# Keeping 15 instead of 12 squared-score blocks per sequence in an attention, FFN and channel-mix kernel

## The chip, the core and the metric

The program runs on one core of a Trainium2 chip. The metric is the device time of one execution in microseconds (us). The engines are TensorE (PE in the profile, its weight loads PEld), VectorE (DVE), ScalarE (ACT), GpSimd (POOL, idle here) and SyncE (SP), which issues almost all DMAs and does it in order: a DMA that waits for an engine holds up every DMA behind it. The time of the kernel before is the median of three runs, 2616.7 us (2616.6 to 2617.11).

## The reference

Three layers follow each other over 4 sequences of 3072 tokens with 256 features; z has 64 features.

```python
scores = scale * np.matmul(z, z.transpose(0, 2, 1))
attn = np.maximum(scores, 0.0) ** 2
out = np.matmul(attn, v)
x = u * out                              # attention
h = x @ w_in
x = (h - np.tanh(h)) @ w_out             # FFN, d_ff 2048
xk = mu_k * x + (1.0 - mu_k) * x_prev    # x_prev: the token before
xr = mu_r * x + (1.0 - mu_r) * x_prev
k = np.maximum(xk @ w_k, 0.0)            # channel mix, d_ff 1024
out = 1.0 / (1.0 + np.exp(-(xr @ w_r))) * (k * k @ w_v)
```

The scores are symmetric: the block of queries g and keys i is the transpose of the block of queries i and keys g.

## The kernel before

**Tiles and units.** Tokens are cut into 24 tiles of 512 (`t`, six for each of the 4 sequences, `g` is the place in the sequence). A unit is a pair of 128-row chunks. The attention has 24 x 12 units `("A", t, p)`, and 12 key pairs `kp` make up six blocks of 512 keys. The units of the FFN (`H`) and of the channel mix (`K`, `R`) follow. Loop `n` does `produce(units[n])` and then `consume(units[n - 2])` (`LAG = 2`).

**Precision.** Every operand is split into a high part `h` (a copy in fp32r by `copy_hi` on ACT or a cast on DVE) and a low part `l` (a subtraction on DVE, `sub_lo`), and a product takes three matmuls.

**A fresh attention unit** takes 4 matmuls into PSUM tile `w` (lines 428 and 429), a Relu (line 339) and a Square (line 340) on ACT into `a`, the high and the low part, and later 12 matmuls into `acc` (line 500).

**A kept unit.** For query tile g the first `min(g, 3)` key blocks are not computed again. The tile with the smaller index stored the squared block (`keep`, line 370, 512 KB for each pair), and `again_load` (line 377) fetches it as four DMAs of 256 KB, 7 units before its first use. `turn` (line 402) turns it with two 32x32-block transposes on DVE, `turned_high` copies the high part on ACT, and the low part follows. Such a unit has no matmuls in `produce`, only the 12 of `consume`. In tiles with g < 3 the query columns stand in another order (`swapped`, `columns`), which costs a copy `zq` of each such z tile.

**What sets the order.** Every engine works in the order in which the program is written. Other work (z, v, u and weight preparation) is cut into steps with a cost, a first and a last unit. `run_steps(n)` puts in as many as a budget `left` allows. The weights come as 64-bit floats and are rebuilt on DVE by `c_steps` during the attention.

**Pools.** Tile tag `p4` has 10 buffers and holds raw loads, u, x1 and weights under way, `e` has 4 and holds `a`, `big` has 12 and holds v, fetched blocks and weights, `hi` and `lo` have 3 each, PSUM `wk` 2.

Of the kernel before, what the change touches and what calls it, by code (L numbers as in the profile page):

```python
# [7 lines left out]
F32 = mybir.dt.float32  # L8
F32R = mybir.dt.float32r
# [10 lines left out]
def relu2_attention__tanh_ffn__channel_mix_kernel(  # L20
# [23 lines left out]


# [13 lines left out]
    AGAIN = 3  # L59
# [39 lines left out]
    zin, z1, zq, z2, vraw, vs, uin, uT = {}, {}, {}, {}, {}, {}, {}, {}  # L99
# [78 lines left out]
    def u_turn(t):  # L178
        a = uin.pop(t)
        w = p4(f"uT{t}")  # L180
        if t % NG < AGAIN:
            for c in range(DC):
                nc.vector.transpose(
                    out=w[:, c].rearrange("p (b a i) -> p b a i", a=4, b=4),
                    in_=a[:, c].rearrange("p (a b) i -> p b a i", a=4),
                )
        else:
            nc.vector.transpose(
                out=w.rearrange("p c t -> p (c t)"), in_=a.rearrange("p c k i -> p (c k i)")
            )  # L190
        uT[t] = w
# [142 lines left out]
    def square_split(name, w, sc, pieces=1, high=nc.vector.tensor_copy, beside=None):  # L334
        a = scratch(f"a_{name}")
        h, l = parts(name)
        for j in range(pieces):
            x = slice(2 * j // pieces, 2 * (j + 1) // pieces)
            nc.scalar.activation(out=a[:, x], in_=w[:, x], func=ACTF.Relu, scale=sc)  # L339
            nc.scalar.activation(out=a[:, x], in_=a[:, x], func=ACTF.Square)  # L340
            if j == 0 and beside:
                beside()
            high(h[:, x], a[:, x])  # L343
            sub_lo(l[:, x], a[:, x], h[:, x])
        return a, h, l


    again = {g: range(min(g, AGAIN)) for g in range(NG)}
    fresh = {g: [j for j in range(NG) if j not in again[g]] for g in range(NG)}
    pairs = {}  # L350
    for g in range(NG):
        of_f = [2 * j + h for j in fresh[g] for h in range(2)]
        of_r = [2 * j + h for j in again[g] for h in range(2)]
        if g == 1:
            of_f = of_f[2:] + of_f[:2]
        if len(of_r) == 2:
            pairs[g] = of_f[:8] + [of_r[0], of_f[8], of_r[1], of_f[9]]
        elif len(of_r) == 4:
            pairs[g] = [x for i in range(4) for x in (*of_f[2 * i : 2 * i + 2], of_r[i])]
        elif of_r:  # L360
            pairs[g] = [x for i in range(6) for x in (of_f[i], of_r[i])]
        else:
            pairs[g] = of_f
# [4 lines left out]
    def keep(b, g, kp, a):  # L368
        rows = kept[b, g, kp // 2][kp % 2 * 2 * P : (kp % 2 + 1) * 2 * P, :]
        nc.sync.dma_start(out=rows.rearrange("(c p) q -> p c q", p=P), in_=a)  # L370

    def again_load(b, g, i):

        t = sb.tile([P, 16, 4 * 32], F32, tag="big", name=f"b{b}_{g}_{i}", bufs=12)
        src = kept[b, i, g].rearrange("(m j) (q x) -> q j m x", j=32, q=4)
        for q in range(4):
            nc.sync.dma_start(out=t[32 * q : 32 * q + 32], in_=src[q])
        blocks[b, g, i] = t

    def is_again(n):  # L380
        if n >= NT * NP:
            return False
        g, q = n // NP % NG, n % NP
        return pairs[g][q] // 2 in again[g]

    def turn(n):
# [5 lines left out]
        x = blocks[b, g, kp // 2]  # L392
        a = scratch(f"t_{t}_{q}")
        for j in range(2):
            f = kp % 2 * 2 + j
            y = x[:, :, f * 32 : f * 32 + 32]
            if g < AGAIN:
                y = y.rearrange("p (c k) i -> p k c i", c=4)
                o = a[:, j].rearrange("p (k c i) -> p k c i", k=4, c=4)
            else:  # L400
                o = a[:, j].rearrange("p (m i) -> p m i", i=32)
            nc.vector.transpose(out=o, in_=y)
        turned[n] = a

    def turned_high(n):
        if n in turned:
            h, l = parts("t_{}_{}".format(*divmod(n, NP)))
            copy_hi(h, turned[n])
            turned[n] = (turned[n], h, l)

    def produce(unit):
# [3 lines left out]
        if n in turned:  # L415
            a, h, l = turned.pop(n)
            sub_lo(l, a, h)
            split[unit] = (h, l)
            return
        w = work(f"w_{name}")  # L420
        if kind == "A":
            turn(n + 1)
            b, g = divmod(t, NG)
            kp = pairs[g][p]
            for j in range(2):
                kc = 2 * kp + j
# [3 lines left out]
            a, *split[unit] = square_split(  # L430
                name, w, scale, 2 if t == 0 and p == 0 else 1,
                copy_hi if g > 1 else nc.vector.tensor_copy, lambda: run_steps(n),
            )
            if (b, g, kp // 2) in kept:
                stores[n + 1] = lambda: keep(b, g, kp, a)
        elif kind in ("H", "K"):
# [15 lines left out]
            if kind == "K":  # L452
                _, *split[unit] = square_split(name, w, 1.0)
# [31 lines left out]
    def consume(unit):  # L485
# [6 lines left out]
        for j in range(2):  # L492
            f = 2 * (pairs[t % NG][p] if kind == "A" else p) + j
# [22 lines left out]
    def x2_steps(i):  # L516
        def f():
            o = acc.pop(("H", i))
            x2t[i] = []
            for c in range(DC):  # L520
                x = p2(f"x2_{i}_{c}")
                if i % NG < AGAIN:
                    nc.scalar.activation(out=columns(x), in_=swapped(o[:, c]), func=ACTF.Copy)
                else:
                    nc.scalar.activation(out=x, in_=o[:, c], func=ACTF.Copy)
# [105 lines left out]
    for b in range(1, B):  # L631
        prev = (b - 1) * NG * NP
        last = prev + (NG - 1) * NP
        for g in range(NG):
            n = prev + (3 + g) * NP if g < 3 else last + 3 + LAG + (1, 2, 5)[g - 3]
            load(n, v_load, b, g)
            task(n + 3, min(n + 12, b * NG * NP + 2 * g + LAG - 2), v_steps, b, g)
        for g in range(NG):
            n = last - 3 * NP // 2 + 3 * g if g < 3 else last + 2 * (g - 3) + 2
            load(n - 3, z_load, b, g)  # L640
            task(n, b * NG * NP + 2 * g - 1 if g else b * NG * NP - 5, z_steps, b, g)
    for t in range(NT):
        b, g = divmod(t, NG)
        for i in again[g]:
            load(t * NP + pairs[g].index(2 * i) - 7, again_load, b, g, i)
    order = [(k, g) for g in range(F1 // 512) for k in ("in", "out")]
    order += [(k, g) for k in ("k", "v") for g in range(F2 // 512)] + [("r", 0)]
    halves = [(k, g, h) for k, g in order for h in range(1 if k == "r" else 2)]
    c0 = NP + 2
    c1 = (NT - NG) * NP  # L650
    for n, x in enumerate(halves):
        k = c0 + n * (c1 - c0) // len(halves)
        load(k - 3, c_load, *x)
        task(k, k + 2 * (c1 - c0) // len(halves), c_steps, *x)
# [22 lines left out]
    def run_steps(n):  # L677
# [20 lines left out]
    with tc.manual_schedule():  # L698
# [10 lines left out]
        for n in range(len(units) + LAG + 3):  # L709
# [8 lines left out]
            turned_high(n + 1)  # L718
# [37 lines left out]
```

## Time and profile before

| | us |
|---|---|
| median of three runs | 2616.7 |
| the profiled execution, its own time | 2616.88 |
| its span, first to last instruction | 2615.1 |
| PE busy | 2595.5 (99%) |
| DVE busy | 1669.4 (64%) |
| ACT busy | 1387.9 (53%) |

The 1.8 us between the span and the time lie around the first and the last instruction. The attention takes the first 980 us or so, in which the DVE is much busier than after it. A busy share is an average, and whether an engine limits the kernel is read from who waits for it.

### The profile page before, as it was taken

How to read it: one execution, taken by the hardware profiler on the slowest of the kernel's cores; microseconds unless marked ns; L12 is line 12 of the kernel's file. 1: busy time of each engine (PE TensorE's matmuls, PEld its weight loads, DVE VectorE, ACT ScalarE, POOL GpSimd, SP SyncE). 2: the span in 40 equal slices, each digit the busy share in tenths (PEclk: the TensorE clock that was granted, in tenths of full speed). 3: DMA queues.
4: the chain of work that ended last, by engine and by line, in shares of the span. 5: the costliest groups of instructions: out<-in, count | busy, mean ns of one | idle time of the engine just before them, and what ended most of it. 6: DMA issues, size and time to landing. Idle time of an engine off the chain costs nothing.

```text
span 2615.1 us, 28460 instructions
## 1 busy us (share of the span) xinstructions
PE 2595.5 (99%) x11424; PEld 2146.2 (82%) x11424; DVE 1669.4 (64%) x1880; ACT 1387.9 (53%) x1502; POOL 0.2 (0%) x4
## 2 busy tenths in 40 slices
PE   8999999999999999999999999999999999999998
PEld 6888888888888888888888888888888888888887
DVE  7888888887886666555555555555555555555554
ACT  6666666656666665444444444444444444444443
POOL 0000000000000000000000000000000000000000
PEclk9999999999999999999999999999999999999999
DMA  8685777578657630000000000000000000000000
GB/s 209 203 211 132 231 196 175 153 205 221 151 162 210 139 112 33 15 12 12 17 15 14 17 17 17 17 17 17 17 17 17 17 17 17 17 17 17 17 9 17
DMA packets 415604, 203.99 MB, mean 78 GB/s; under 512 B 261488, under 2 KB 372080, under 8 KB 415472
## 3 DMA queue, kind: packets, MB, share of 16 engines
q1 hardware_dynamic: 414416, 202.04, 30.3%
q8 instruction: 89, 1.46, 0.2%
q14 instruction: 43, 0.35, 0.0%
q10 hardware_dynamic: 1056, 0.13, 0.0%
HBM read 114.03 MB, written 82.05 MB: 75 GB/s over the span
## 4 chain that ended last, share of the span: by engine, by line
PE 99%; DVE 1%; ACT 0%; DMA 0%; issue 0%; ACTq 0%; DVEq 0%
PE acc_A L500 30%; PE acc_H L500 20%; PE w_H L444 20%; PE acc_K L500 10%; PE w_K L444 10%; PE w_A L428 3%; PE w_A L429 3%; PE w_R L468 2%; DVE z L96 0%; DMA zin<-in_z_dram 0%; DVE zt L118 0%; ACT zq L93 0%; DVE l_A L96 0%; ACT h_A L93 0%; DVE z L119 0%
## 5 line engine op out<-in xcount | busy, mean ns | idle before, releaser
L500 PE MATMUL acc_A<-h_A,v 128*128 128x512 f32 x1536 | 504.0, 390 | 0.0
L500 PE MATMUL acc_H<-h_H,w_out 128*128 128x512 f32 x1536 | 504.0, 389 | 0.0
L444 PE MATMUL w_H<-xh,w_in 128*128 128x512 f32 x1536 | 500.4, 389 | 0.0
L93 ACT ACTIVATE h_H<-g_H 128x1024 fp32r<-128x1024 f32 x192 | 203.7, 1061 | 386.3 <-DVE g_H L458 386.3
L96 DVE TENSOR_TENSOR l_H<-g_H,h_H 128x1024 fp32r<-128x1024 f32 x192 | 235.4, 1226 | 216.3 <-ACT h_H L93 216.3
L339 ACT ACTIVATE a_A<-w_A 128x1024 f32<-128x1024 f32 (+1 forms) x193 | 197.7, 1024 | 300.3 <-PE w_A L429 294.1
L458 DVE TENSOR_TENSOR g_H<-w_H,g_H 128x1024 f32<-128x1024 f32 x192 | 233.6, 1217 | 171.3 <-ACT g_H L457 171.3
L500 PEld LDWEIGHTS acc_A<-h_A,v 128*128 128x128 f32 x1536 | 289.1, 188 | 60.1
L500 PEld LDWEIGHTS acc_H<-h_H,w_out 128*128 128x128 f32 x1536 | 288.3, 188 | 59.8
L444 PEld LDWEIGHTS w_H<-xh,w_in 128*128 128x128 f32 x1536 | 288.3, 188 | 59.8
L457 ACT ACTIVATE g_H<-w_H 128x1024 f32<-128x1024 f32 x192 | 195.8, 1020 | 243.3 <-PE w_H L444 243.1
L96 DVE TENSOR_TENSOR l_A<-a_A,h_A 128x1024 fp32r<-128x1024 f32 (+1 forms) x193 | 235.4, 1219 | 128.7 <-ACT h_A L93 125.1
L500 PE MATMUL acc_A<-l_A,v 128*128 128x512 f32 x768 | 299.9, 391 | 0.0
L444 PE MATMUL w_H<-x,w_in 128*128 128x512 f32 x768 | 298.8, 389 | 0.0
L500 PE MATMUL acc_H<-l_H,w_out 128*128 128x512 f32 x768 | 298.8, 389 | 0.0
L500 PE MATMUL acc_A<-h_t,v 128*128 128x512 f32 x768 | 252.0, 389 | 0.0
L444 PE MATMUL w_K<-mkh,w_k 128*128 128x512 f32 x768 | 251.8, 389 | 0.0
L500 PE MATMUL acc_K<-h_K,w_v 128*128 128x512 f32 x768 | 251.8, 389 | 0.0
L340 ACT ACTIVATE a_A<-a_A 128x1024 f32<-128x1024 f32 (+1 forms) x193 | 204.0, 1057 | 6.1
L343 DVE CAST h_K<-a_K 128x1024 fp32r<-128x1024 f32 x96 | 66.7, 695 | 212.8 <-ACT a_K L340 212.8
L339 ACT ACTIVATE a_K<-w_K 128x1024 f32<-128x1024 f32 x96 | 98.8, 1029 | 136.8 <-PE w_K L444 134.5
L500 PEld LDWEIGHTS acc_A<-l_A,v 128*128 128x128 f32 x768 | 144.6, 188 | 32.3 <-DVE l_A L96 2.1
(127 smaller groups left out, 3484.6 us busy)
## 6 DMA issues: line engine op xcount, KB each, us to landing
at<-a_A SPq DMA_DIRECT2D x96, 512.0 KB, 3.4
b<-at SPq DMA_DIRECT2D x192, 256.0 KB, 4.8
vr<-in_v_dram SPq DMA_DIRECT2D x24, 512.0 KB, 5.5
uin<-in_u_dram SPq DMA_DIRECT2D x192, 64.0 KB, 2.7
x1d<-x SPq DMA_DIRECT2D x24, 512.0 KB, 3.1
x<-x1d SPq DMA_DIRECT2D x24, 512.0 KB, 3.8
out_dram<-ot SPq DMA_DIRECT2D x192, 64.0 KB, 1.9
zin<-in_z_dram SPq DMA_DIRECT2D x94, 64.0 KB, 2.7
```

The lines of the kernel that those rows point to most:

```text
L93: nc.scalar.activation(out=o, in_=i, func=ACTF.Copy)
L96: nc.vector.tensor_tensor(out=o, in0=i, in1=hi.bitcast(F32), op=ALU.subtract)
L339: nc.scalar.activation(out=a[:, x], in_=w[:, x], func=ACTF.Relu, scale=sc)
L340: nc.scalar.activation(out=a[:, x], in_=a[:, x], func=ACTF.Square)
L343: high(h[:, x], a[:, x])
L428: nc.tensor.matmul(w[:, j], lhsT, zq[b, g], start=True, stop=False)
L429: nc.tensor.matmul(w[:, j], lhsT, z2[t], start=False, stop=True)
L444: nc.tensor.matmul(w[:, j], ws[wt, f // 4][a][:, c, (f % 4) * P : (f % 4 + 1) * P], x[m][:, c], start=n == 0, stop=n == 3 * DC - 1,)
L457: nc.scalar.activation(out=g, in_=w, func=ACTF.Tanh)
L458: nc.vector.tensor_tensor(out=g, in0=w, in1=g, op=ALU.subtract)
L468: nc.tensor.matmul(w[:, d], ws["r", 0][a][:, c, d * P : (d + 1) * P], x[m][:, c], start=n == 0, stop=n == 3 * DC - 1,)
L500: nc.tensor.matmul(o[:, c], w[a][:, c * P : (c + 1) * P], s[m][:, j], start=p == 0 and j == 0 and n == 0, stop=p == last and j == 1 and n ...
```

## The change

For query tile g all g lower blocks are now kept, 15 instead of 12 for a sequence. The tile that computes a block turns it with two DVE transposes into a `p4` tile and stores that, so that a fetch brings rows of 1 KB to a group of 32 partitions. The user of a block does no transposes: ACT copies the high part and DVE subtracts, each as two instructions of 512 columns. A pair `kp` now stands for chunks 0 and 2 or 1 and 3 of a block. The swapped column order and the `zq` copies are gone. The sequence of fresh and kept units is written as strings, fetches go out 5 units ahead instead of 7, the high cast stands on ACT more often, loads and steps of z, v and weights have other places, and the weight conversion spreads over more of the attention.

```diff
-    AGAIN = 3
+    AHEAD = 5
...
-    kept = {(b, i, g): dr.tile([TB, TB], F32, name=f"at{b}_{i}_{g}")
-            for b in range(B) for g in range(NG) for i in again[g]}
-    stores, blocks, turned = {}, {}, {}
...
+        ("ffffffffffff", "ffffrfrfffff", "ffrffrffrffr", "frfrfrfrfrfr", "rfrrfrrfrrfr", "rrfrrrrrfrrr")
...
+    kept = {(b, i, g): dr.tile([2 * P, 1024], F32, name=f"at{b}_{i}_{g}")
+            for b in range(B) for g in range(NG) for i in range(g)}
...
+    def keep(n, b, g, kp, a):
...
+        t = p4(f"k{b}_{g}_{kp}", shape=(P, 4, 4, 2, 32))
+        for c in range(2):
+            nc.vector.transpose(
+                out=t[:, :, :, c].rearrange("p b a j -> p a b j"),
+                in_=a[:, c].rearrange("p (a b i) -> p a b i", a=4, b=4),
+            )
...
+        def store():
+            rows = kept[b, g, kp // 2][kp % 2 * P : (kp % 2 + 1) * P, :]
+            nc.sync.dma_start(out=rows, in_=t.rearrange("p b a c j -> p (b a c j)"))
+            stored.add((b, g, kp))
...
+        stores[n + 1] = store
...
+        t = sb.tile([P, 8, 256], F32, tag="big", name=f"b{b}_{g}_{i}", bufs=12)
+        src = kept[b, i, g].rearrange("(m i) (q x) -> q i m x", i=32, q=4)
...
+        for hj, lj, xj in turned[n][0]:
+            copy_hi(hj, xj)
...
+            for hj, lj, xj in views:
+                sub_lo(lj, xj, hj)
...
-                nc.tensor.matmul(w[:, j], lhsT, zq[b, g], start=True, stop=False)
+                nc.tensor.matmul(w[:, j], lhsT, z1[b, g], start=True, stop=False)
...
+            def beside(a):
+                run_steps(n)
+                if kept_on:
+                    keep(n, b, g, kp, a)
...
+                nc.vector.tensor_copy if n < 3 or not g and p % 3 == 2 else copy_hi, beside,
...
+        left = {"A": 2.0, "H": 2.2, "K": 2.4, "R": 4.0}[kind] + spare[0]
+        if kind == "A":
+            t, q = divmod(n, NP)
+            j = pairs[t % NG][q] // 2 - t % NG
+            left -= 1.0 if j < 0 else 1.1 if j > 0 else 0.0
```

On DVE, in the first tile at units 3 and 4, the program before has a cast and a subtraction for each unit and the preparation of a z tile between them (`a`, `h`, `l` are the squared scores and their parts, the last number but one is the unit):

```order
L343 CAST h_A_3_270<-a_A_3_269 128x1024
L96 TENSOR_TENSOR l_A_3_271<-a_A_3_269,h_A_3_270 128x1024
L118 STREAM_TRANSPOSE zt_4_304<-zin_4_258 128x512
L119 CAST z_0_4_305<-zt_4_304 128x512
L96 TENSOR_TENSOR z_0_4_305<-zt_4_304,z_0_4_305 64x512
L343 CAST h_A_4_300<-a_A_4_299 128x1024
L96 TENSOR_TENSOR l_A_4_301<-a_A_4_299,h_A_4_300 128x1024
```

The same place in the changed program, `k` being the turned tile that is stored:

```order
L341 STREAM_TRANSPOSE k_0_3_286<-a_A_3_278 128x4x4x32 x2
L87 TENSOR_TENSOR l_A_3_280<-a_A_3_278,h_A_3_279 128x1024
L341 STREAM_TRANSPOSE k_0_4_316<-a_A_4_311 128x4x4x32 x2
L87 TENSOR_TENSOR l_A_4_313<-a_A_4_311,h_A_4_312 128x1024
L109 STREAM_TRANSPOSE zt_4_358<-zin_4_267 128x512
L110 CAST z_0_4_359<-zt_4_358 128x512
L87 TENSOR_TENSOR z_0_4_359<-zt_4_358,z_0_4_359 64x512
```

Two transposes have taken the place of the cast ahead of each subtraction, and two casts in three have gone to ACT.

On DVE, in the second tile, which uses the first kept block `b`, the program before turns it (`t`) and subtracts:

```order
L402 STREAM_TRANSPOSE t_8_763<-b_1_0_582 128x512 x2
L183 STREAM_TRANSPOSE uT_775<-uin_573 128x512 x2
L343 CAST h_A_7_771<-a_A_7_770 128x1024
L96 TENSOR_TENSOR l_A_7_772<-a_A_7_770,h_A_7_771 128x1024
L96 TENSOR_TENSOR l_t_8_793<-t_8_763,h_t_8_792 128x1024
```

In the changed program a kept unit (`l_t`) is two subtractions, and the fresh units beside it have the transposes:

```order
L341 STREAM_TRANSPOSE k_1_5_691<-a_A_3_682 128x4x4x32 x2
L87 TENSOR_TENSOR l_A_3_684<-a_A_3_682,h_A_3_683 128x1024
L87 TENSOR_TENSOR l_t_4_709<-b_1_0_547,h_t_4_708 128x512 x2
L218 TENSOR_SCALAR c_r_0_552<-cw_r_0_687 128x512
L221 TENSOR_TENSOR cw_r_0_687<-cw_r_0_687,c_r_0_552 128x512
L222 TENSOR_SCALAR cw_r_0_687<-cw_r_0_687 128x512
L341 STREAM_TRANSPOSE k_1_6_740<-a_A_5_732 128x4x4x32 x2
L87 TENSOR_TENSOR l_A_5_734<-a_A_5_732,h_A_5_733 128x1024
```

The transposes have moved from the tile that uses a block to the tile that computes it.

On ACT, at the very start of the program before, the three copies `zq` stand among the first unit's Relu (line 339) and Square (line 340):

```order
L93 ACTIVATE zq_0_162<-z_0_0_158 128x512
L93 ACTIVATE z_0_164<-zt_0_157 64x512
L93 ACTIVATE zq_1_172<-z_0_1_168 128x512
L93 ACTIVATE v_0_174<-vr_0_148 128x1024
L339 ACTIVATE a_A_0_186<-w_A_0_181 128x512
L340 ACTIVATE a_A_0_186<-a_A_0_186 128x512
L93 ACTIVATE zq_2_196<-z_0_2_192 128x512
L339 ACTIVATE a_A_0_186<-w_A_0_181 128x512
L340 ACTIVATE a_A_0_186<-a_A_0_186 128x512
```

In the changed program they read:

```order
L84 ACTIVATE z_0_174<-zt_0_169 64x512
L84 ACTIVATE v_0_182<-vr_0_160 128x1024
L318 ACTIVATE a_A_0_194<-w_A_0_189 128x512
L319 ACTIVATE a_A_0_194<-a_A_0_194 128x512
L318 ACTIVATE a_A_0_194<-w_A_0_189 128x512
L319 ACTIVATE a_A_0_194<-a_A_0_194 128x512
L318 ACTIVATE a_A_1_220<-w_A_1_215 128x1024
```

The second half of the first unit's Relu (line 318 now) no longer stands behind a copy of the third z tile. On PE the changed program has 96 matmuls fewer.

## Rows read from the trace of the kernel before

**Rows 1.** The page, parts 1 and 4: engines, and the chain by engine.

```profile
PE 2595.5 (99%) x11424; PEld 2146.2 (82%) x11424; DVE 1669.4 (64%) x1880; ACT 1387.9 (53%) x1502; POOL 0.2 (0%) x4
...
PE 99%; DVE 1%; ACT 0%; DMA 0%; issue 0%; ACTq 0%; DVEq 0%
```

**Rows 2.** Who waited for whom, PE: total us, times, longest.

```profile
PE w_A L428 <- ACT zq L93: 6.8, 1, 6.8
PE w_A L428 <- ACT a_A L339: 4.7, 1, 4.7
```

**Rows 3.** Busy us by stretch (engines as above); then PE's clock, DMA share, GB/s.

```profile
400.00:600.00 200.00, 200.00 (x882) 165.22 (x881) 172.72 (x228) 129.41 (x127) 0.00 (x0) 1.00 0.68 182
...
1000.00:2600.00 1600.00, 1600.00 (x7060) 1324.85 (x7060) 870.07 (x874) 730.34 (x854) 0.00 (x0) 1.00 0.07 15
```

**Rows 4.** Groups by line and shape, ACT, first 960 us: busy, mean ns.

```profile
L340 ACT ACTIVATE a_A<-a_A 128x1024 f32<-128x1024 f32 x190 | 201.7, 1062 | 6.0
L339 ACT ACTIVATE a_A<-w_A 128x1024 f32<-128x1024 f32 x190 | 195.5, 1029 | 298.1 <-PE w_A L429 291.9 <-DMA uin<-in_u_dram 4.5 <-DVE h_A L343 1.5
L93 ACT ACTIVATE h_A<-a_A 128x1024 fp32r<-128x1024 f32 x102 | 108.0, 1059 | 2.7
```

**Rows 5.** Instructions in order of time, ACT: start, us.

```profile
10.83 0.58 ACT L339 ACTIVATE a_A<-w_A 128x512 f32<-128x512 f32 x1
11.44 0.63 ACT L340 ACTIVATE a_A<-a_A 128x512 f32<-128x512 f32 x1
14.02 0.63 ACT L93 ACTIVATE zq<-z 128x512 fp32r<-128x512 f32 x1 [1.95 <-DVE z L96]
14.55 0.58 ACT L339 ACTIVATE a_A<-w_A 128x512 f32<-128x512 f32 x1
```

**Rows 6.** The same view, DVE.

```profile
16.29 0.69 DVE L96 TENSOR_TENSOR l_A<-a_A,h_A 128x512 fp32r<-128x512 f32 x1
...
43.03 1.30 DVE L183 STREAM_TRANSPOSE uT<-uin 128x512 f32<-128x512 f32 x2
...
49.14 1.23 DVE L96 TENSOR_TENSOR l_A<-a_A,h_A 128x1024 fp32r<-128x1024 f32 x1
50.29 0.69 DVE L343 CAST h_A<-a_A 128x1024 fp32r<-128x1024 f32 x1
```

**Rows 7.** Instructions in order of time: SP, and PE after the first tile.

```profile
35.86 8.52 SPq L172 DMA_DIRECT2D uin<-in_u_dram  x8
...
61.20 0.39 PE L428 MATMUL w_A<-zq,z 128*128 128x512 f32 x1
```

**Rows 8.** The view of rows 3, stretches of tiles 0, 2, 5 and 6.

```profile
0.00:61.20 61.20, 49.70 (x200) 40.27 (x201) 46.05 (x60) 38.65 (x41) 0.20 (x4) 0.94 0.81 206
...
102.00:141.90 39.90, 39.90 (x178) 33.03 (x176) 27.73 (x34) 28.39 (x28) 0.00 (x0) 1.00 0.91 244
...
218.10:257.10 39.00, 39.00 (x172) 31.89 (x172) 33.96 (x44) 26.88 (x27) 0.00 (x0) 1.00 0.51 129
257.10:300.60 43.50, 43.50 (x194) 36.02 (x193) 38.06 (x48) 27.92 (x28) 0.00 (x0) 1.00 0.56 183
```

**Rows 9.** The view of rows 4, DVE.

```profile
L96 DVE TENSOR_TENSOR l_A<-a_A,h_A 128x1024 fp32r<-128x1024 f32 x189 | 231.5, 1225 | 128.1 <-ACT h_A L93 124.6 <-PE w_A L429 0.3
L402 DVE STREAM_TRANSPOSE t<-b 128x512 f32<-128x512 f32 x190 | 123.3, 687 | 0.0
...
L343 DVE CAST h_A<-a_A 128x1024 fp32r<-128x1024 f32 x87 | 60.1, 690 | 44.8 <-ACT a_A L340 44.2
...
L183 DVE STREAM_TRANSPOSE uT<-uin 128x512 f32<-128x512 f32 x24 | 15.5, 686 | 0.0
```

**Rows 10.** The page, part 6: DMA issues, KB each, median us to landing.

```profile
at<-a_A SPq DMA_DIRECT2D x96, 512.0 KB, 3.4
```

**Rows 11.** DMAs of block tile b, first 960 us; last line from issue to landing.

```profile
L377 SPq DMA_DIRECT2D b<-at x192: 302/487/2052, 58.9 to 928.0; - x192
...
DMA to landing us min/median/max: 3.0/4.8/7.7
```

More of the change, by code (lines that the diff above doesn't have):

```diff
@@ L180, in u_turn @@
         w = p4(f"uT{t}")
[L181 to L190, printed above, removed]
+        nc.vector.transpose(
+            out=w.rearrange("p c t -> p (c t)"), in_=a.rearrange("p c k i -> p (c k i)")
+        )
         uT[t] = w
@@ L340, in square_split @@
             nc.scalar.activation(out=a[:, x], in_=a[:, x], func=ACTF.Square)
-            if j == 0 and beside:
-                beside()
+            if j == pieces - 1 and beside:
+                beside(a)
             high(h[:, x], a[:, x])
             sub_lo(l[:, x], a[:, x], h[:, x])
-        return a, h, l
-    again = {g: range(min(g, AGAIN)) for g in range(NG)}
-    fresh = {g: [j for j in range(NG) if j not in again[g]] for g in range(NG)}
+        return h, l
     pairs = {}
[L351 to L363, printed above, removed]
@@ L364, in relu2_attention__tanh_ffn__channel_mix_kernel @@
-    kept = {(b, i, g): dr.tile([TB, TB], F32, name=f"at{b}_{i}_{g}")
-            for b in range(B) for g in range(NG) for i in again[g]}
-    stores, blocks, turned = {}, {}, {}
-    def keep(b, g, kp, a):
-        rows = kept[b, g, kp // 2][kp % 2 * 2 * P : (kp % 2 + 1) * 2 * P, :]
-        nc.sync.dma_start(out=rows.rearrange("(c p) q -> p c q", p=P), in_=a)
+    for g, order in enumerate(
+        ("ffffffffffff", "ffffrfrfffff", "ffrffrffrffr", "frfrfrfrfrfr", "rfrrfrrfrrfr", "rrfrrrrrfrrr")
+    ):
+        left = {"r": list(range(2 * g)), "f": list(range(2 * g, NP))}
+        pairs[g] = [left[x].pop(0) for x in order]
@@ new lines, in relu2_attention__tanh_ffn__channel_mix_kernel @@
+    kept = {(b, i, g): dr.tile([2 * P, 1024], F32, name=f"at{b}_{i}_{g}")
+            for b in range(B) for g in range(NG) for i in range(g)}
+    stores, stored, blocks, turned = {}, set(), {}, {}
+    def keep(n, b, g, kp, a):
+        t = p4(f"k{b}_{g}_{kp}", shape=(P, 4, 4, 2, 32))
+        for c in range(2):
+            nc.vector.transpose(
+                out=t[:, :, :, c].rearrange("p b a j -> p a b j"),
+                in_=a[:, c].rearrange("p (a b i) -> p a b i", a=4, b=4),
+            )
+        def store():
[3 more added lines that the diff above has]
+        stores[n + 1] = store
@@ L372, in again_load @@
     def again_load(b, g, i):
[L374 to L375 removed]
+        assert {(b, i, 2 * g), (b, i, 2 * g + 1)} <= stored
+        t = sb.tile([P, 8, 256], F32, tag="big", name=f"b{b}_{g}_{i}", bufs=12)
+        src = kept[b, i, g].rearrange("(m i) (q x) -> q i m x", i=32, q=4)
         for q in range(4):
@@ L380, in is_again, with again_high @@
     def is_again(n):
[L381 to L386, printed above, removed]
+        return n < NT * NP and pairs[n // NP % NG][n % NP] // 2 < n // NP % NG
+    def again_high(n):
         if not is_again(n):
@@ L391, in turn @@
         kp = pairs[g][q]
[L392 to L409, printed above, removed]
+        x = blocks[b, g, kp // 2].rearrange("p m (a c j) -> p a c m j", c=2, j=32)
+        h, l = parts(f"t_{t}_{q}")
+        turned[n] = [
+            [y[:, j].rearrange("p (c m j) -> p c m j", c=2, j=32) for y in (h, l)]
+            + [x[:, kp % 2 + 2 * j]]
+            for j in range(2)
+        ], (h, l)
+        for hj, lj, xj in turned[n][0]:
+            copy_hi(hj, xj)
     def produce(unit):
@@ L415, in produce @@
         if n in turned:
-            a, h, l = turned.pop(n)
-            sub_lo(l, a, h)
-            split[unit] = (h, l)
+            views, split[unit] = turned.pop(n)
+            for hj, lj, xj in views:
+                sub_lo(lj, xj, hj)
             return
@@ L521, in f @@
                 x = p2(f"x2_{i}_{c}")
[L522 to L525, printed above, removed]
+                nc.scalar.activation(out=x, in_=o[:, c], func=ACTF.Copy)
                 x2t[i].append(x)
@@ L653, in relu2_attention__tanh_ffn__channel_mix_kernel @@
         load(k - 3, c_load, *x)
-        task(k, k + 2 * (c1 - c0) // len(halves), c_steps, *x)
-    first = [c1 + NP // 2 + n * (NG - 2) * NP // 4 for n in range(3)]
+        task(k, k + (c1 - c0) // len(halves) + 2, c_steps, *x)
     last = (NT - 1) * NP + LAG
-    slots = first + [last + x for x in (3, 5, 6, 7, 9, 10, 11, 13, 14)]
+    slots = [last + x for x in (-30, -18, 3, 6, 6, 9, 9, 11, 11, 12, 13, 14)]
     for n, (kind, g) in enumerate(order):
-        k = first[-1] + 3 if kind == "r" else slots[n] + 2
+        k = slots[1] + 3 if kind == "r" else slots[n] + 2
         load(k - 2, w_load, kind, g)
```

55 lines of the change are left out of this document (21 added, 34 removed).

## The prediction

> **What bounds the kernel now.** I read the page first. PE is busy 99% of the span, the chain that ended last is 99% PE, and DVE and ACT have 64% and 53% [rows 1]. Then the waits of PE: two, 11.5 us together, both in the first 16 us [rows 2]. So from there to the tail no other engine ever makes PE wait, and a matmul taken out should shorten the program by its own step. The step is read from stretches, because a matmul's own duration overlaps its neighbour's: 1600 us hold 7060 matmuls in the FFN and channel mix, 0.2266 us each, and 200 us hold 882 in the attention, 0.2268 us each [rows 3]. The reader should see that the attention already runs at the pace of the stage that has nothing to wait for. What the table of stretches adds is how near the others are there: DVE is busy 172.7 of 200 us in the attention and the DMA share is 0.68 [rows 3], so those two are what the change can push over the edge.
>
> **What it removes.** Three more blocks in each of 4 sequences are 12 blocks, 24 units, 4 score matmuls each: 96 x 0.2268 = 21.8 us off PE. The Relu and the Square of those 24 units go too (24 x 2.09 us of ACT [rows 4]), and 12 copies `zq`.
>
> **The start.** PE's second wait (4.7 us [rows 2]) ends when the second half of the first Relu ends. That half began at 14.55 behind the third `zq`, which began at 14.02 [rows 5]. Without `zq` it follows the first Square, which began at 11.44 and takes 0.63 [rows 5], and the v copy ahead of all this is not held by a `zq` either. PE goes on 2.5 us earlier by this (14.55 to 12.07), and up to 3.8 with two `zq` of 0.63 gone from ahead of that v copy. The first unit's last subtraction, 16.29 to about 17.0 [rows 6], still stands behind the third z tile's steps on DVE and comes some 1.7 us earlier, at about 15.3.
>
> That lead does not last, because DVE sets the pace of the first tile. Back to back it steps by less than its durations: 1.15 us for a 1024-wide subtraction (49.14 to 50.29) and 0.65 us for a 512-wide transpose (two in 1.30) [rows 6]. From 15.3 to the last subtraction of the tile the order holds 11 subtractions (12.7), 20 transposes for `k` (13.0), 5 casts (3.6), 3 z tiles of 1.9 (5.6), 5 low parts of v (5.8), one turned u tile of 1024 (1.2): 41.9 us with two trifles, so 57.2. PE's last 12 matmuls of the tile follow, 2.7 us, to 59.9. Before they ended at 61.2 [rows 7]. The term is -1.3 us. If PE kept its whole lead, it would be -3.8. If DVE idles as it does now in this stretch (46.05 busy of 61.2 [rows 8], some 7 us of the 15 after the first unit), it is +5.
>
> **The first tile of the other sequences.** Here every unit is fresh and ten of twelve are stored. PE has 12 x 16 x 0.2268 = 43.5 us, as the row of that tile shows [rows 8]. On DVE the changed order has 12 subtractions (13.8), 20 transposes (13.0), 4 casts (2.8), 4 low parts of v (4.6), 10 steps of weight conversion (5.5), one u tile and one product with u (2.4): 42.1 us at the back-to-back steps, 44.2 by the mean durations [rows 9]. Now it has 38.1 [rows 8]. So DVE goes to 97 or 101% of PE. The slack of one unit hides that: from the end of a unit's score matmuls, Relu 1.03, Square 1.06 [rows 4], two transposes 1.3, subtraction 1.15 make 4.5 us, and PE needs the result after two units' `consume` and two `produce`, 2 x 3.63 = 7.26. 2.7 us of slack against an excess between -1.4 and +0.7: I take 0. The bound is +2.5 for each of three such tiles, if the slack is already spent on weight steps that stand ahead of the transposes.
>
> ACT does three passes in most such units, 3.15 us [rows 4] against PE's 3.63, and some copies of v: 36.8 us against 43.5, no bound.
>
> **The later tiles.** A kept unit costs DVE two 512-wide subtractions (0.69 each [rows 6]) instead of two transposes and a 1024-wide one: 1.4 for 2.6 us. In the last tile of a sequence (10 kept units, 36.3 us of PE) the changed order has 29.8 us of DVE work; before it was 34.0 in 39.0 [rows 8]. ACT copies 2 x 0.63 [rows 5] instead of 1.05. The weight steps between two kept units take up to 3.0 us of a 2.72-us unit, some 3 us of lag at the worst place and gone a unit or two later: 0 to +1 a sequence, I take 0.5 in all.
>
> **DMA.** Stored and fetched together are now 5 MB a tile everywhere (before 5, 5, 5, 3, 3, 3). The shares that 5 MB gave were 0.56 in a first tile and 0.91 at most, at 244 GB/s, with no PE wait [rows 8]; a fetch is 4 x 256 packets of 1 KB instead of 4 x 512 of 512 B, so 0.9 is again the most I expect. A store waits for two transposes more than before. Its `p4` buffer is wanted again three units later (10.9 us) at five places and two units later (7.3 us) at one, and a store takes 3.4 us to land [rows 10]: I take 0, and what it could cost is a DVE wait that belongs to the first rival.
>
> A fetch lands 4.8 us after its issue in the median [rows 11]. If the four fetches of a block followed each other, a block would take 19.2 us and the three of a last tile 57.6 us of its 39.0; that tile shows no PE wait and a DMA share of 0.51 [rows 2, 8], so they overlap, and the sum goes by that. The Trainium skill speaks against it: by "SBUF — State Buffer", section "Door 1: The DMA port swizzle (why `[64,N]` ≈ `[32,N]`)", a transfer to 32 partitions, as each of these is, reaches 8 of 16 ports, and by its section "Can I just issue two DMAs to hit both halves?" two such transfers serialize. By that rule five blocks of a last tile would come one fetch at a time and the kernel would end at the third rival's time; by the rows nothing is added.
>
> **The sum.** The profiled execution was 2616.9 us: -21.8 - 1.3 + 0.5 gives 2594.3, and the median of the runs is 0.2 lower: **2594 us**.
>
> **Rivals.**
>
> *DVE sets the pace of the first tiles.* For it: 97 to 101% in those tiles and a DVE order that puts steps, transposes and cast ahead of each subtraction. Against it: 2.7 us of slack. Price by the bounds: +6.3 in the first tile and 2.5 in each of three others, up to 14 us: 2597 to 2608. A long PE wait would also cost clock: around the two waits of the start the granted clock was 0.94 of full in the first 61.2 us and 1.00 later [rows 8]. Chance 0.13.
>
> *Blocks come late.* The lead falls from 7 units to 5. PE needs a block 7 units after the fetch is issued, 7 x 2.72 = 19 us in a last tile, less 2.6 for copies and subtractions: 16.4. Against that stand a store ahead in SP's queue that waits up to a unit (3.6), four issues of 0.49 and at most 7.7 to land [rows 11], and for the third-next block of the last tile eight u issues that once took 8.5 us [rows 7]: 13 to 22 us. Only the worst of everything is late, 5 us for one block a sequence, behind it ACT and all fresh units. 2596 to 2614, chance 0.08.
>
> *The fetches of a block do not overlap.* At 19.2 us a block, the five of a last tile take 96 us against 36.3 of PE. Each sequence would lose 60 us, 2594 + 4 x 60 = some 2830, slower. The three blocks of the last tile before speak against it, as worked out above. Chance 0.01.
>
> *Turning into a permuted place is dear.* The new transposes write runs of 32 columns 64 or 256 columns apart, which no row shows on the writing side. Transposes that permute on the reading side take 686 and 687 ns [rows 9], the nearest rows, and that is the value I take; a gain is excluded, since each still passes 512 columns. At twice the price (1.30 us) first tiles lack 8.9 us, second tiles (16 transposes) 6.6, third tiles 2.3, 17.8 a sequence, +71: 2665, slower. It decides from about 1.05 us a transpose, where first and second tiles together lose 5.8 us in each sequence and eat the gain. Chance 0.03.
>
> **How the numbers follow.** The likeliest, with its own range 2591 to 2598 (the two bounds of the start, 0 to 2 us of lag later), has 0.75, the others 0.13, 0.08, 0.01 and 0.03. The range 2590.5 to 2603 adds the lower half of the two middle rivals and leaves out about 0.15. A difference of 0.2% (5.2 us) is about what a measurement of this kernel can tell from no change. Faster by more than that (below 2611.5): 0.75 + 0.13 + most of 0.08, less a little for what I have not seen, 0.93. Within it 0.03: late blocks at their worst, or a transpose near 1.05 us. Slower 0.04.
>
> **What would show it.** Right: 11328 matmuls, 96 fewer; no PE wait after the first 20 us or only traces; second Relu half of the first unit at about 11 to 12 us; line 341's transposes at about 0.69 us; DVE busy about 42 of 43.5 us in the stretches of the first tiles. Wrong: PE waits for `l_A` (line 87) in tiles 0, 6, 12, 18, which is the first rival; for `h_t` (line 84) with ACT waiting for a DMA, the second; line 341 at over 1 us, the last. A DVE wait for the store of a `k` tile would show that the `p4` pool, which I put at 0, is a wait of its own.

## The result and the profile after

The changed kernel takes 2594.89 us (median of 4 runs, 2593.08 to 2595.9), the kernel before 2616.65 on the same chip (4 runs, 2616.6 to 2617.11). The ratio is 0.9916, 95% interval 0.9898 to 0.9933: 21.8 us faster, against 2594.0 forecast. The profiled execution took 2593.08 us, its span 2591.3.

The page, parts 1, 4, 5 and 6; the rows that answer to it are [rows 1], [rows 9] and [rows 10]:

```profile
PE 2572.6 (99%) x11328; PEld 2127.7 (82%) x11328; DVE 1656.8 (64%) x1966; ACT 1417.3 (55%) x1632; POOL 0.2 (0%) x4
...
PE 98%; DVE 1%; ACT 0%; SPq 0%; issue 0%; DMA 0%; DVEq 0%
...
L341 DVE STREAM_TRANSPOSE k<-a_A 128x512 f32<-128x512 f32 x240 | 156.2, 689 | 83.7 <-ACT a_A L319 83.3
...
at<-k SPq DMA_DIRECT2D x120, 512.0 KB, 3.3
b<-at SPq DMA_DIRECT2D x240, 256.0 KB, 5.9
```

PE has 96 matmuls fewer and is still the chain. A transpose that writes into permuted places takes 689 ns, as one that permutes what it reads did [rows 9]. A fetch lands later than before, 5.9 us against 4.8 [rows 11].

Who waited for whom, PE, all of its waits (total us, times, longest), as in [rows 2]:

```profile
PE w_A L396 <- DVE z L87: 6.0, 1, 6.0
PE acc_A L476 <- DVE v L87: 1.8, 3, 1.1
PE acc_A L476 <- DVE l_A L87: 1.0, 2, 0.8
PE w_A L396 <- ACT a_A L318: 0.9, 1, 0.9
PE acc_A L476 <- DVE head L693: 0.5, 1, 0.5
PE acc_A L476 <- DVE h_A L322: 0.4, 1, 0.4
```

All of them lie before 55 us. The wait of 4.7 us behind the first unit has become 0.9. PE in order of time shows it:

```profile
9.50 0.53 PE L397 MATMUL w_A<-z,z 128*128 128x512 f32 x1
10.92 0.50 PE L396 MATMUL w_A<-z,z 128*128 128x512 f32 x1 [0.89 <-ACT a_A L318]
```

The second Relu half, forecast at 11 to 12 us, begins at 10.29 in the same view of ACT:

```profile
10.29 0.58 ACT L318 ACTIVATE a_A<-w_A 128x512 f32<-128x512 f32 x1
```

Stretches of tiles 0, 3, 4, 5 and 6 (columns as in [rows 3]; before, [rows 8]):

```profile
0.00:60.67 60.67, 50.07 (x201) 38.15 (x201) 52.16 (x70) 44.08 (x46) 0.20 (x4) 1.00 0.82 213
141.36:179.44 38.08, 38.08 (x169) 31.56 (x168) 30.17 (x45) 24.56 (x30) 0.00 (x0) 1.00 0.94 234
179.44:214.82 35.38, 35.38 (x157) 29.26 (x156) 28.76 (x43) 21.87 (x30) 0.00 (x0) 1.00 1.00 249
214.82:251.09 36.27, 36.27 (x162) 30.02 (x160) 28.20 (x42) 20.83 (x28) 0.00 (x0) 1.00 0.83 200
251.09:294.61 43.52, 43.52 (x194) 36.06 (x192) 40.32 (x52) 37.00 (x37) 0.00 (x0) 1.00 0.66 205
```

From tile 1 on, PE is busy in the whole of each stretch. Two loads differ from the forecast. DVE has 40.3 us in the first tile of a sequence, not 42.1. The DMA share is 0.94 in the fourth tile and 1.00 in the fifth, where I expected 0.9 at most. ACT waits for no block in these two. It does wait for blocks, four times, but all in last tiles (at 231, 474, 699 and 709 us), and PE does not notice:

```profile
ACT h_t L84 <- DMA b<-at: 11.4, 4, 3.3
```

**Where the 23.8 us of span came from.** I read it off the start times of PE's matmuls. Those removed are 96 x 0.2267 = 21.8. PE starts at 6.00 and not 6.78 us: 0.8. The steps longer than 0.30 us sum to 10.4 us over the usual step before and 9.1 after (called the excess below): 1.3. That last part is not in the first tile (9.0 before, 9.1 after). Before, it was five places between 193 and 693 us, some 0.26 each, where a weight load waited for a low part; this is the row of PE's weight loads before:

```profile
PEld acc_A L500 <- DVE l_A L96: 2.1, 5, 0.5
```

After, there are none.

### The profile page after: what moved, and what is told of

Same layout as the page of the kernel before. It is cut to its first block, busy times and chain, and to the rows that moved or that the text cites. A ratio compares the mean times of both kernels' runs of the same rounds, so it can differ in the third digit from the quotient of the medians.

```text
span 2591.3 us, 28822 instructions
## 1 busy us (share of the span) xinstructions
PE 2572.6 (99%) x11328; PEld 2127.7 (82%) x11328; DVE 1656.8 (64%) x1966; ACT 1417.3 (55%) x1632; POOL 0.2 (0%) x4
## 4 chain that ended last, share of the span: by engine, by line
PE 98%; DVE 1%; ACT 0%; SPq 0%; issue 0%; DMA 0%; DVEq 0%
PE acc_A L476 29%; PE acc_H L476 20%; PE w_H L417 20%; PE acc_K L476 10%; PE w_K L417 10%; PE w_A L397 3%; PE w_A L396 3%; PE w_R L441 3%; DVE v L87 0%; SPq L99 0%; DMA vr<-in_v_dram 0%; ACT v L84 0%; ACT a_A L318 0%; SPq L158 0%; DVE k L341 0%
## 5 line engine op out<-in xcount | busy, mean ns | idle before, releaser
L476 PE MATMUL acc_A<-h_A,v 128*128 128x512 f32 x1344 | 441.0, 390 | 2.2 <-DVE v L87 1.8
L476 PE MATMUL acc_A<-h_t,v 128*128 128x512 f32 x960 | 310.1, 389 | 0.0
L476 PEld LDWEIGHTS acc_A<-h_A,v 128*128 128x128 f32 x1344 | 252.2, 188 | 56.2 <-DVE v L87 3.0
L318 ACT ACTIVATE a_A<-w_A 128x1024 f32<-128x1024 f32 (+1 forms) x169 | 172.7, 1022 | 194.1 <-PE w_A L397 193.9
L476 PE MATMUL acc_A<-l_A,v 128*128 128x512 f32 x672 | 262.2, 390 | 1.5 <-DVE l_A L87 1.0
L87 DVE TENSOR_TENSOR l_A<-a_A,h_A 128x1024 fp32r<-128x1024 f32 (+1 forms) x169 | 201.4, 1192 | 56.5 <-ACT h_A L84 55.7
L476 PEld LDWEIGHTS acc_A<-h_t,v 128*128 128x128 f32 x960 | 180.3, 188 | 37.3
L341 DVE STREAM_TRANSPOSE k<-a_A 128x512 f32<-128x512 f32 x240 | 156.2, 689 | 83.7 <-ACT a_A L319 83.3
L476 PE MATMUL acc_A<-l_t,v 128*128 128x512 f32 x480 | 186.9, 389 | 0.0
```

The lines of the kernel that those rows point to most:

```text
L87: nc.vector.tensor_tensor(out=o, in0=i, in1=hi.bitcast(F32), op=ALU.subtract)
L341: nc.vector.transpose(out=t[:, :, :, c].rearrange("p b a j -> p a b j"), in_=a[:, c].rearrange("p (a b i) -> p a b i", a=4, b=4),)
L476: nc.tensor.matmul(o[:, c], w[a][:, c * P : (c + 1) * P], s[m][:, j], start=p == 0 and j == 0 and n == 0, stop=p == last and j == 1 and n ...
```

## The experiments

Each comparison is with the kernel before on the same chip (2616.6 to 2616.7). Where another time is named, it is the changed kernel run again (the control, on the chip of experiments 1 to 3):

> The changed kernel itself once more, to have its time on the same chip as the next three. Both theories: 2593 to 2596 us, no PE wait after the first tile. Should a wait of PE turn up later than 61 us, it tells which wait makes its runs differ by 2.8 us where the kernel before differs by 0.5.

2593.66 us (2593.34 to 2593.86, 4 runs), ratio 0.9911 (0.9898 to 0.9925). Its excess over the usual step is 9.6 us, and all but 0.2 of it in the first tile.

**1. The rearrangement with 12 blocks.** The block lists are cut to the first three, the rest stays.

```diff
-"frfrfrfrfrfr", "rfrrfrrfrrfr", "rrfrrrrrfrrr"
+"frfrfrfrfrfr", "frfrfrfrfrfr", "frfrfrfrfrfr"
...
-    left = {"r": list(range(2 * g)), "f": list(range(2 * g, NP))}
+    left = {"r": list(range(2 * min(g, 3))), "f": list(range(2 * min(g, 3), NP))}
...
```

> Only 12 blocks kept as before, everything else as changed (layout, turning by the computing tile, no zq, casts, fetches 5 units ahead). Theory 1, the gain is the 96 matmuls and a little at the start: 2594.9 + 96 x 0.2267 = 2616.7 us, 2615 to 2618. Theory 2, the rearrangement of the other engines' work carries a good part of the gain: 2612 us or less.

2614.96 us (2614.78 to 2615.4, 11 runs), ratio 0.9993 (0.9984 to 1.0002). The twelve blocks are worth 2614.96 - 2593.66 = 21.3 us, the rest of the change 1.7. So the gain is the 96 matmuls, nearly one for one.

**2. The first tile without its transposes.** The 20 transposes of tile 0 are left out and the squared scores stored unturned, so the blocks fetched from them are wrong.

```diff
-        t = p4(f"k{b}_{g}_{kp}", shape=(P, 4, 4, 2, 32))
-        for c in range(2):
+        plain = b == 0 and g == 0
+        t = a if plain else p4(f"k{b}_{g}_{kp}", shape=(P, 4, 4, 2, 32))
+        for c in range(0 if plain else 2):
...
```

> In the first tile alone the ten stored pairs are stored as they are, without the 20 transposes (13 us of DVE), so blocks with the first tile come out unturned and the output is not the reference's. Theory 1, DVE's amount of work sets the pace of the first tile: PE's gaps there (about 6 us of waits after 10 us) close, 2589 to 2590.5 us. Theory 2, those gaps come from late loads of v and z or from the order, not from the amount: within 1 us of the control.

2592.39 us (2591.71 to 2593.16, 4 runs), ratio 0.9907 (0.9893 to 0.992): 1.3 us, not 3 to 5. The stretch of the first tile in this run, columns as in [rows 3]:

```profile
0.00:58.80 58.80, 49.85 (x201) 38.20 (x202) 40.79 (x50) 44.13 (x46) 0.20 (x4) 1.00 0.88 228
```

DVE has 40.8 us of work instead of 52.2, 11.4 less, and the tile ends 1.9 us earlier (its excess over the usual step is 7.3 us instead of 9.1); 1.2 us of that are lost again at 242 and 704 us. DVE's work is not without effect: in the changed kernel it leaves DVE no pause from 9.3 to 44.1 us, where PE has most of its small waits, and without the transposes it does. The same stretch in the changed kernel and in this run:

```profile
9.27:44.14 34.87, 30.96 (x128) 23.38 (x127) 34.29 (x48) 27.16 (x29) 0.00 (x0) 1.00 0.76 200
...
9.27:44.14 34.87, 32.49 (x136) 24.80 (x135) 26.86 (x35) 29.12 (x32) 0.00 (x0) 1.00 0.90 248
```

But PE's own work is close behind: 201 steps of 0.2267 are 45.6 us, the start 6.0 and the excess 9.1, together 60.7, and only 1.9 of that hang on these transposes.

**3. The same transposes, put off.** Those of pairs 4 to 8 of the first tile go to units 13 and later, from a buffer of their own.

```diff
+                if put_off:
+                    first = 13 + 2 * (kp - 4)
+                    insert(first, first + 4, lambda: [(1.3, lambda: keep(now[0], b, g, kp, a))])
...
```

> The turning of pairs 4 to 8 of the first tile (6.5 us of DVE) is put off into the second and third tile, where DVE has 6 us and 9 us to spare; nothing is left out. Theory 1: the gaps after 26 us in the first tile (about 2.9 us) go, 2591.5 to 2593 us, no new PE wait in the second tile. Theory 2: within 1 us of the control.

2593.1 us (2592.8 to 2593.76, 4 runs), ratio 0.991 (0.9896 to 0.9923): 0.6 us less than the control, no more than two runs of one kernel differ by. This agrees with experiment 2.

**4. The three `zq` copies back at the start.** The first three z tiles are copied on ACT again and the matmuls read the copies.

```diff
...
+            if b == 0 and g < 3:
+                zq[b, g] = q = p2(f"zq_{b}_{g}", F32R)
+                copy_hi(q, w.bitcast(F32))
...
-nc.tensor.matmul(w[:, j], lhsT, z1[b, g], start=True, stop=False)
+nc.tensor.matmul(w[:, j], lhsT, zq[b, g], start=True, stop=False)
```

> The copies zq of the first three z tiles are back, with nothing else changed. Theory 1, they cost the start 2.4 us of DVE's lead and PE's long wait comes back, and with it the stretch of half clock: 2596 to 2598.5 us, the granted clock of the first tile at 0.94 again. Theory 2, the pace of DVE in the first tile hides the start: within 1 us of the control, 2594 to 2596.

2598.36 us (2596.59 to 2602.5, 5 runs), ratio 0.9932 (0.992 to 0.9945): 4.7 more than the control. In its profiled execution (span 2594.8, 3.3 over the control's) PE starts at 6.50 instead of 5.82, and the excess is 12.3 us. ACT does its copies ahead of v again:

```profile
5.81 0.63 ACT L84 ACTIVATE zq<-z 128x512 fp32r<-128x512 f32 x1 [0.56 <-DVE z L87]
8.52 0.63 ACT L84 ACTIVATE zq<-z 128x512 fp32r<-128x512 f32 x1 [2.07 <-DVE z L87]
9.05 1.04 ACT L84 ACTIVATE v<-vr 128x1024 fp32r<-128x1024 f32 x1
...
14.27 0.63 ACT L84 ACTIVATE zq<-z 128x512 fp32r<-128x512 f32 x1 [1.88 <-DVE z L87]
...
16.80 1.04 ACT L84 ACTIVATE v<-vr 128x1024 fp32r<-128x1024 f32 x1
```

The second of these copies of v in the control:

```profile
13.55 1.04 ACT L85 ACTIVATE v<-vr 128x1024 fp32r<-128x1024 f32 x1
```

DVE's subtraction for that v, in this run:

```profile
17.88 1.23 DVE L87 TENSOR_TENSOR v<-vr,v 128x1024 fp32r<-128x1024 f32 x1 [2.46 <-DMA vr<-in_v_dram]
```

So the copies delay the start, as theory 1 had it. The third one waits for its z tile with ACT's other work behind it, and ACT copies the second v 3.25 us later than in the control. DVE subtracts right after that copy, at 17.88 and not 14.63, and from there the kernel stays 3.3 us behind. (The view puts DVE's wait down to the v load, but that load left at 7.0 us in the control and at 7.1 here, and the wait ends with ACT's copy.) The granted clock of 0.94 that theory 1 also named is not there: it reads 1.00 in the first 61.2 us, and PE's steps of 0.427 us up to 15 us stand in the control as well. The time of the other four runs is 1.6 to 5.9 us longer still, and no trace shows why.

**5. Rows of 512 bytes.** The block is stored as two rows of 2 KB for each partition and fetched in rows of 512 bytes, as large as before the change.

```diff
-dr.tile([2 * P, 1024], F32
+dr.tile([4 * P, 512], F32
...
-shape=(P, 4, 4, 2, 32)
+shape=(P, 2, 4, 4, 32)
...
```

> Packets of the kernel before (fetches in rows of 512 B, stores in rows of 2 KB) with everything else as changed. Theory 1, the 1-KB rows are what keeps the DMA just able to feed the fourth and fifth tile of each sequence, whose share is already 0.94 to 1.02: at twice the packets the fetches of a fifth tile take some 5.7 us more of 35.4, blocks come late and PE waits, 5 to 8 us a sequence, 2610 to 2625 us. Theory 2, the DMA has room in time even at a share of 1: 2594 to 2597 us.

2593.4 us (2593.1 to 2593.7, 4 runs), ratio 0.9911 (0.9898 to 0.9925): no difference. The fifth tile's stretch has a DMA share of 1.05 for 1.00:

```profile
179.44:214.82 35.38, 35.38 (x158) 29.24 (x157) 28.41 (x43) 22.22 (x30) 0.00 (x0) 1.00 1.05 245
```

A fetch lands after 5.3 us and not 5.9:

```profile
b<-at SPq DMA_DIRECT2D x240, 256.0 KB, 5.3
```

The 1-KB rows are not what makes 15 blocks possible.

**6. A lead of three units.** `AHEAD = 3`.

> Fetches go out 3 units ahead instead of 5. Theory 1, what is left of the lead is a few us: PE needs a block 5 units after the issue, 13.6 us less 2.6, against 9 us of landing at most and up to 4 of issuing, so several blocks of the later tiles are late by 1 to 5 us: 2600 to 2625 us, with ACT waiting for the fetch. Theory 2, the lead has room: 2594 to 2597 us.

2615.57 us (2611.48 to 2618.93, 11 runs), ratio 0.9998 (0.9989 to 1.0006): the whole gain is gone. ACT's waits for blocks in this run:

```profile
ACT h_t L84 <- DMA b<-at: 62.5, 19, 8.6
```

PE's waits in this run, two of its rows:

```profile
PE acc_A L476 <- DVE l_A L87: 6.0, 5, 1.7
...
PE acc_A L476 <- ACT h_t L84: 5.1, 4, 2.3
```

The stretch in which sequence 0 has its last tile in the changed kernel:

```profile
214.82:251.09 36.27, 32.62 (x126) 25.50 (x125) 23.40 (x36) 15.07 (x22) 0.00 (x0) 0.91 0.94 218
```

Late blocks cost more than the wait: PE's granted clock is 0.91 there, and after a step of 2.1 us at 229 us and one of 0.7 at 231 seven matmuls step by 0.427 us before 0.227 is back.

**7. Lead four, lead seven.** `AHEAD = 4` and `AHEAD = 7`.

> The lead of the fetches is 4 units. At 5 ACT waited 11.4 us for blocks, 3.3 us at most, and PE not at all; at 3 it waited 62.5 us, 8.6 at most, and the gain was lost. Theory 1, the slack at 5 is less than one unit (2.7 us): ACT's longest wait is 6 to 7 us, PE waits 1 to 3 us at one place in each sequence, 2596 to 2604 us. Rival, there is more than a unit to spare: 2593 to 2595 us.

2614.71 us (2610.8 to 2617.58, 11 runs), ratio 0.9991 (0.9983 to 1.0). ACT waited longer than theory 1 had it, and the time is outside its range.

```profile
ACT h_t L84 <- DMA b<-at: 51.4, 13, 8.4
```

The reason is not the 2.7 us of one unit. With the shorter lead a fetch also changes its place in SP's queue. SP at the third block of sequence 0's last tile, at a lead of four:

```profile
213.34 4.18 SPq L158 DMA_DIRECT2D uin<-in_u_dram  x8
...
219.76 1.91 SPq L358 DMA_DIRECT2D b<-at  x4
```

The same in the control:

```profile
208.50 2.76 SPq L359 DMA_DIRECT2D b<-at  x4
...
213.36 5.84 SPq L159 DMA_DIRECT2D uin<-in_u_dram  x8
```

The fetch stood ahead of the eight u issues and stands behind them now, and leaves 11.3 us later. In sequences 1 and 2 it is some 14 us, beyond what the kernel lags by then. At a lead of three it leaves at 221.34, only 1.6 us later again, which fits that three and four cost the same. So these two runs show what a place in the queue is worth, and not how much time is to spare at five.

> The lead of the fetches is 7 units, as before the change, and not 5. Theory 1, at a lead of 5 no block is late enough to hold PE, although ACT waits 11.4 us for fetches: no gain, 2593 to 2595 us; ACT's wait for b is gone. Rival: part of the small waits of ACT is passed on to PE in most executions, a gain of 1 to 3 us. Under both, SP's queue should show the same stores.

2598.78 us (2596.3 to 2599.62, 5 runs), ratio 0.993 (0.9917 to 0.9942): 5.1 us slower than at five. Both theories were wrong. DVE's waits for z in this run:

```profile
DVE zt L109 <- DMA zin<-in_z_dram: 19.0, 6, 6.3
```

The same row of the control:

```profile
DVE zt L110 <- DMA zin<-in_z_dram: 4.7, 3, 3.9
```

Now the z tiles of the next sequence are late. In the last tile of sequence 2, SP in order of time:

```profile
688.37 8.52 SPq L158 DMA_DIRECT2D uin<-in_u_dram  x8
696.94 2.08 SPq L99 DMA_DIRECT2D zin<-in_z_dram  x4
```

And DVE there:

```profile
695.18 1.29 DVE L87 TENSOR_TENSOR l_t<-b,h_t 128x512 fp32r<-128x512 f32 x2 [0.29 <-ACT h_t L84]
702.79 0.71 DVE L109 STREAM_TRANSPOSE zt<-zin 128x512 f32<-128x512 f32 x1 [6.31 <-DMA zin<-in_z_dram]
```

The same z load left at 688.59 in the control, where DVE did not wait for it at all. Here DVE stands before the z tile for 6.3 us, the low parts `l_t` of the next kept unit stand behind it, and PE stops at 703.4 for 1.8 us. One reason is in SP's waits: its fetches wait 7.5 us for buffers that DVE still reads (line 358, `DVE l_t`), which they never do at five. How much of the delay that makes was not separated.

**8. Low part first.** In a stored unit the low part is subtracted before the two transposes.

```diff
-                run_steps(n)
-                if kept_on:
-                    keep(n, b, g, kp, a)
+                run_steps(n)
...
-            split[unit] = square_split(
+            a, *split[unit] = square_split(
...
+            if kept_on:
+                keep(n, b, g, kp, a)
...
```

> The low part of a unit is subtracted before the unit's two transposes instead of after them, nothing left out. Theory 1, DVE's amount sets the pace and the order only shifts one unit's transposes: each low part is 1.3 us earlier once, 0.5 to 1.5 us faster than the control, 2593 to 2594.5. Theory 2, the order is the cause of PE's gaps in the first tile: they close, 2589 to 2591.

2601.07 us (2597.77 to 2603.44, 5 runs), ratio 0.994 (0.9927 to 0.9954): 7.4 us slower. PE's excess is 17.0 us, 9.2 in the first tile as without the edit and 7.8 in the last tiles of sequences 0 to 2. SP and ACT in that of sequence 0, in order of time:

```profile
209.86 0.80 SPq L348 DMA_DIRECT2D at<-k  x1
...
213.95 7.68 SPq L158 DMA_DIRECT2D uin<-in_u_dram  x8
...
224.38 1.86 SPq L358 DMA_DIRECT2D b<-at  x4
...
233.39 1.15 ACT L84 ACTIVATE h_t<-b 128x512 fp32r<-128x512 f32 x2 [5.42 <-DMA b<-at]
```

The same in the control:

```profile
207.71 0.69 SPq L349 DMA_DIRECT2D at<-k  x1
...
221.96 1.86 SPq L359 DMA_DIRECT2D b<-at  x4
...
230.91 1.15 ACT L85 ACTIVATE h_t<-b 128x512 fp32r<-128x512 f32 x2 [2.87 <-DMA b<-at]
```

A subtraction ahead of the transposes delays the store by 2.15 us, and the fetch right behind it in SP's queue by 2.3. At the u issues only 0.6 us of that is left, but they take 7.7 us and not 5.8 (experiment 7 has the control's row), so the next fetch leaves 2.4 us later and ACT gets the block 2.5 us later. Why they take longer was not tested; they now begin 0.9 us behind the fetch ahead of them, before 2.1. A wait of 2.9 us costs PE nothing; one of 5.4 holds DVE for 4.9 us behind it, and PE for 1.9.

**9. Low part first, lead seven.** Both edits together.

> The low part is subtracted before the transposes, as in the run that gave 2601.07 us, with a lead of 7 units. Theory 1, what cost 7.4 us there was that each store stood some 2 us later in SP's queue and the fetches of the last tiles behind it, so that blocks came late: the four gaps of PE in tile 5 of the sequences (7.7 us over the usual step) go, the 1.2 us in the first tile stay, 2594 to 2596 us. Rival, the order on DVE itself costs it: no change from 2598 to 2602 us.

2602.99 us (2598.78 to 2605.52, 5 runs), ratio 0.9945 (0.9933 to 0.9958). The longer lead does not bring the time back, so by my own test theory 1 fell. The rival does not follow either, since the trace has another wait in its place, that of experiment 7:

```profile
DVE zt L109 <- DMA zin<-in_z_dram: 20.7, 5, 7.8
```

**10. More work for DVE in the first tiles of sequences 1 to 3.** Half of the low part is subtracted twice in the ten stored units.

```diff
             sub_lo(l[:, x], a[:, x], h[:, x])
+        if more:
+            sub_lo(l[:, 0], a[:, 0], h[:, 0])
...
```

> In the ten stored units of the first tile of sequences 1 to 3 half of the low part is subtracted a second time (30 more subtractions of 512, 0.69 us each, 0.65 back to back). DVE then has 40.3 + 6.5 = 46.8 us of work in a tile that gives PE 43.5. Theory 1, DVE's lag has only the 2.7 us of one unit's slack: 0.6 to 3.3 us for each of three tiles, 2595.5 to 2603.5 us, with PE waiting for l_A there. Rival, the lag is made up in kept units of the next tile and PE never sees it: 2593 to 2595 us.

2606.31 us (2605.91 to 2607.66, 5 runs), ratio 0.9962 (0.9949 to 0.9976): 12.6 us over the control, above theory 1's range. In the trace PE falls 3.6, 3.6 and 4.4 us behind the control in the three first tiles, and another 1.1 in the last tiles of sequences 1 and 2. The first tile of sequence 1:

```profile
251.10:297.20 46.10, 44.01 (x189) 34.73 (x188) 43.98 (x60) 36.15 (x36) 0.00 (x0) 1.00 0.60 191
```

PE's waits for low parts:

```profile
PE acc_A L478 <- DVE l_A L87: 7.1, 12, 1.2
```

6.5 us more work cost 3.6 to 4.4 us a tile: the reserve in such a tile is 2.1 to 2.9 us, a little less than the 3.2 between DVE's 40.3 and PE's 43.5, and the slack of one unit adds nothing to it.

## Why the prediction was right

**Removed matmuls, -21.8.** Right. The count is 11328, the step 0.2267, and experiment 1 prices the blocks at 21.3. This term is most of the sum. The two small ones below missed in opposite directions, by 0.8 and 1.8 us, so that the sum came within 1 us is in part luck.

**The start, -1.3.** Mis-sized: the tile ends at 60.7 us, 0.5 earlier. That PE goes on earlier is right: 0.9 us of waiting for ACT where there were 4.7, and its first matmul comes 0.8 us earlier too, which had no term. The lead has about its forecast size, 2.5 to 3.8: the copies put back cost 3.3 us in the trace (experiment 4). "DVE sets the pace of the first tile" is right from 9.3 to 44.1 us, where DVE has no pause. The control shows it as well: PE's steps are 0.427 us there from 11.6 to 14.6 us, and yet the tile ends within 0.1 us of the changed kernel's first run, since PE waits less afterwards. What was missed is how near PE's own work is: 11.4 us of DVE work less bring the tile's end forward by only 1.9 (experiment 2). The lead is taken back in a row of small waits of PE for v, `l_A`, `h_A` and the mixing constants between 13 and 55 us, in steps of up to 1.5 us, each with a slow step of 0.3 to 0.7 behind it. 3.3 less 1.9 would leave 1.4 us; where the other 0.9 went was not separated.

**First tiles of the other sequences, 0.** Right, with a thinner margin than its reason said. DVE was at 40.3 of 43.5 us, and I had added the 2.7 us of a unit's slack to that. Experiment 10 shows that no more than those 3.2 us are there to spend. By its reserve of 2.1 to 2.9 us, the first rival would begin at about 3 us more DVE work a tile (an estimate).

**Later tiles, +0.5.** Mis-sized: no lag came, and five stalls of the kernel before went, -1.3; they stand in the row of PE's weight loads, which the forecast did not use. The steps between two kept units fill 1.8 us at most, not 3.0: a kept unit of the last tile takes 1.0 off the budget of 2.0 (`run_steps`), so I misread it.

**DMA, 0.** Right for the time, wrong for the load: the share reached 1.00 in the fifth tile, where fetches of blocks, stores and the next sequence's v and z overlap. I had taken 0.9 over from a tile with the same 5 MB. The rows agree that fetches to 32 partitions overlap: 20 fetches of 5.9 us one after the other would be 118 us, and the last tile takes 36.3. By the Trainium skill, "SBUF — State Buffer", section "Can I just issue two DMAs to hit both halves?", two such transfers serialize. Read as the prediction read it, one landing before the next begins, the measurement decides against it; how much bandwidth two of them share, on which the page rests it, was not measured here.

**Late blocks, chance 0.08.** The forecast "only the worst of everything is late" held for the time, but the margin was smaller than it read. ACT waits up to 3.3 us for a block (4.2 in the control, which costs PE 0.2), 5.4 us stop PE for 1.9, and a fetch that leaves 2.4 us later costs 2.3 to 3.1 us a sequence (experiment 8). Counting the lead in units missed that one unit less puts a fetch behind the u issues, which costs the whole gain (experiment 7). What I had not foreseen either is the other side, that a fetch sent earlier displaces z loads in SP's queue (experiment 7).

**Permuted transposes, chance 0.03.** 689 ns, as taken. DVE nowhere waits for the store of a `k` tile, so the `p4` pool is no wait of its own.

Open: how far SP's order alone limits the lead. The eight u issues held SP for 8.5 us [rows 7] and stand ahead of both z loads and fetches; issuing them from another engine wasn't tried. No version measured is faster than the changed kernel by more than its runs differ.

## What to carry to other kernels

Where PE waits for nobody, a removed matmul gives back its own step and nothing else has to be explained; the work of the forecast lies in showing that no other engine or queue comes to the edge. For an engine, compare its work with PE's in the tightest stage and don't add buffer slack to the difference. For a queue that issues in order, a prefetch has a lead that is too short and one that is too long; look at what stands ahead of it in the queue rather than at the lead in units, and moving an instruction that a store waits for moves the fetches behind that store.

## What was not expected of the hardware

- A DMA share of 1.00 to 1.05 over a whole tile, at 245 to 249 GB/s, made PE wait nowhere in that tile. The median landing time of all fetches in these two runs was 5.9 and 5.3 us, for 4.8 before.
- Fetches in 512-byte rows landed sooner than those in 1-KB rows (5.3 us in the median for 5.9), and neither changed the time.
- A step of 2.1 us in PE's work (229 us, lead of three) and one of 0.7 right behind it were followed by seven matmuls at 0.427 us, half the clock. A step of 2.1 us at 703 us (lead of seven) was followed by one of 0.34 and then by steps of 0.227. The longest gap alone did not tell which place costs clock.
